# Which engine issues a load: 22 input loads move from SyncE's queue to ScalarE's in a recurrent-attention and mixer kernel

## The chip, the core and the metric

The kernel runs on one core of a Trainium2 chip. The metric is device time in microseconds of one execution, the median of several runs. Engines are named as in the profile: PE is TensorE's matmul, PEld its weight loads, DVE is VectorE, ACT is ScalarE, POOL is GpSimd, SP is SyncE. A q behind a name (SPq, ACTq) means the engine's sequencer.

## What is computed

Gated linear attention with a decay per key channel, then a mixer: a low-rank mix over the sequence with a residual, and a two-layer MLP with a residual. Inputs are float32, the output is float32 of shape 4 x 768 x 384.

```python
# q, k, v, alpha: (4 batches, 8 heads, 768 steps, 48 channels)
state = np.zeros((B, H, D, D))
for t in range(S):
    state = alpha[:, :, t, :, None] * state + einsum('bhd,bhe->bhde', k[:, :, t], v[:, :, t])
    y[:, :, t] = einsum('bhd,bhde->bhe', q[:, :, t], state)
x = y.transpose(0, 2, 1, 3).reshape(B, S, H * D)          # (4, 768, 384)
h = x.transpose(0, 2, 1) @ U @ V                          # U 768 x 32, V 32 x 768
u = x + h.transpose(0, 2, 1)
out = u + np.maximum(u @ w_ch1, 0) @ w_ch2                # w_ch1 384 x 1536, w_ch2 1536 x 384
```

## The kernel before

The sequence of each batch is cut in chunks of 128 steps, six to a batch. A unit "b.c" is chunk c of batch b; in batch 0 (all six) and batch 1 (the first four) two chunks are handled together as a pair, four heads at a time, and unit b.c is then one half of the heads of a pair. Each unit has four loads of 192 KB, one each of alpha, k, q and v, into one of 40 buffers of the pool io. For a unit:

- ACT takes the logarithm of alpha (L353, L524), PE sums it along the chunk with a triangular matrix (L362 to L369, L531 to L533), and ACT takes exp of the sum and of its negative (L376, L377, L541, L542; results aa, ai) and of the chunk's total (tot: L378, L544).
- k times ai and q times aa (rkq: L384, L552, on POOL or DVE) are transposed on PE (L401, L565) and copied to SBUF (kqt: L264 on ACT, L266 on DVE); in batch 3 a transposing DMA from SP does both (L577).
- PE makes the scores (L425, L593), DVE masks them (pm: L436, L603). v is cast to bf16 (rv: L264, L268). PE makes the state's update from rk and rv (L459, L616), DVE or POOL add and scale it (L474, L488, L627, L643), and PE makes y from scores and state (L498, L508, L655, L660).

Then the mixer of a batch runs: U and V (L675, L689), the sum u (L690), its transposes (L709, or a DMA from SP, L695), the first MLP matmuls (L738) with relu on ACT or DVE (L748, L750), the second (L764), the last sum (L770) and the stores (L773, L775). Weights are loaded and cast in pieces (L296, L264, L268).

The order of all this is written out. `Plan.add` collects some 1,050 operations with what each reads and writes. `TABLE` then lists them in the order in which they are emitted, three characters each: two for the operation's number and one for the engine (P PE, A ACT, D DVE, G POOL, S SP); "++B" is one matmul without use, which keeps PE running. `SLOTS` gives each buffer its place at first use. So every engine runs a fixed list in the table's order, and it waits where the next instruction of its list must wait, whatever stands behind it. All DMAs stand on SP's list: loads, stores and transposes, in the table's order. `Plan.run` calls each operation with its engine's name; a load ignores that name:

```python
P.add(f"load {b}.{c}", lambda e: nc.sync.dma_start(t(), src[b, :, sl, :].rearrange("h t d -> t h d")), w=[t])
```

The framework sets the semaphores. Each DMA gets one of eight landing semaphores in turn, in the order of emission; a DMA that takes a semaphore again waits until the DMA that had it before, eight places earlier, has landed.

At the start ACT loads its function table (L177) ahead of its first Ln. The first loads on SP's list are alpha 0.0, alpha 0.1, alpha 0.3, alpha 0.5, v 0.1, k 0.3, k 0.0, q 0.0, alpha 0.2, k 0.1, v 0.0, q 0.1.

Of the kernel before, what the change touches and what calls it, by code (L numbers as in the profile page):

```python
# [15 lines left out]
TABLE = """
A8SCcACePCfACgA++BBASCzABISDjA++BBQSETABDS++BBJSA9SA+SCiGBESCjG++BC0AChA++BC1PC2AC3ABBS++BA-SDlPDmADnADKA++BBCSCkPABSC5G
ClPCnABMSDoAEVPEXA++BC6DCmDBKSDCPDMPC4ABRSCdABLSBFSDOABUSAFGDPABSSD8ADDDC7PC9DCrPCsDBOSCoPDEPEWAC8PBHSCpDD+PC+ABNSCtPCqD
CvPCuDBGSDNADpGDrPC-PDqDCwPEZGDtADQGDkGDBDEbPEYAAJPDsPBTSDFDDyPGTAAKAEBACyADADDzPDuDD0DEaGEAAD-ADvPDxDAGPEcPAHAD1PEdDDGP
BWSDwDEeADHPDIDEDGEFPEHACxDGVPD2DDLGBYSBVSBPSGXADZPDaPDbDEfPECGDcPDRGGYAEUGDSPBXSDJDEEPD4PEiPEgDGWADdDALGDTPDUAAASD3PD5P  # L20
EhDEjPBcSEGADVAGaGD6AEIPGqAEkDEKDDWPElPDXDGZGBZSD7AGsPDePEmPGUGDfPELPD9AGtADYDEnPEoAEJDEMPENDDgPBaSDiAEpDBgSGbPGdAEOPBbS
GcPGeDEPPEQPERDGiPGjDDhAAOSADGAQSESAGfPAMSGgDEqPErPGwGHBAGvAGuAEsAHDPHGAGkDHFAE7PGhDE5PGyPGmPE8DE1PAWSGxGGnPHEAEtPEzPASS
G0AAUSE6DAeSE2DGzPAiSGrGE9PBdSAgSHaAAPGGoAEvPE0DE+AARGG1DGpAEuDBhSHcPHdAHeAEwDE3PBeSG2PE4DANGG5PExPG6DBkSFXPAYSBiSAcSG3D
G7DFYDFZPAXAAaSG4DFbPBfSATGEyAFcAFBPFCAAVGFdPFeAFJPFHPAhGFhPFKDFDPHHGAfAFiDAjAFRPFaAFFPFIABoSFVPFWAG8DHfAHJPHLAHIDHgDFGD
FSAE-PHiPHkDFfPHhGFEDFgDHKPHzAFtPAdAFrPBmSBlSBjSAoSFADHMAFuAAZABqSHjPHlDG9PG+PG-DAmSHAAHNPHPDAbGHCGAqSGlGHmPHQPAkSFsAAsS
H1PH3ABpSH5AFnPHRDHSGFLPHoDIJAH4AAuSAwSFjPH2AHODH7GFpPFkDAySILPFMDIMAINABnSHnDFPPH9PH-DHTDH6GFNPHbAFoAFqAH8PH+DFlPFmABrS
FQAFODHVPArAHWPHXPHpPHqDApGHYDA4SIAPHuPHZDIBDIPGIRPFTPAnGHrGAlAIOGHvPFvPHsDAtAHtDICDITDFUAF1PGHPIQPISDACSGNPIUPA2SA0SAzA
HwPAvGAxGGOPA6SHxAGBPIWDHUGIVDH0AAEGIDPB8SIHPIIAIKAIEDIFDGIPF2PB0SIGDIXPHyAA5AFwPIYAIZPGCPIaAIhPBwSIjPA3GBsSIbPA1GIiDIkD
B4SA7GGPPGDPIcDBvSIdPIeDFxPIpPIqDBtSGQDGEDGJPKTAKVPLSAInPKWAJ-AB+SIoDIlPIfPImACCSIgDKoAF3PF4DIrPIsDKBPKCABuSGKDKGDIzPB6S
BySKqPKAAI0AKuAJFPFyDKXAAIGKDAB1SJVPJWAIxPKbGKHGJGAJPPJQAKZAJDPCASJJPK9AJKABzSJEAJXPIyDJLPJMAKFAKEAI3PI7PKYAI8AI4AKrAJbP  # L30
JBPKUGKPPJYAI1PKsAK-PLBAB9SJZPLUPB2SJcDKtABxSKdPKQDLnAJRPJaAI-PLDAJSAKwGI2DKvDLAAJCDKaGLXAJHPJIDCESLYAJAAItPLVALZGIuAIvP
IwAKxPKzDKIPI5PKKDLWAI6ANWALCACGSI9PKyPI+AKJPKfDK0AKjPKkDKcPB3SJjPJkPB7SKLDLFGKMPLaGKeACBSKlGK+GKODK1PK2DKgPKiDJlPLpPLqA
NYPK3DNaANbAKpGB5SCDSF7PF8PB-SNeGLEGLbPJNPNcAKNDNZAKhDK4PLrALtGK7PLdALcPLsDK5DK6GCFSLeAF9PLHPLuPLJDCMSJOAKmPCISF+DLNPLwA
LODCUSK8AJTPJUALGPLIDLvPNdGLxACYSLPGCQSKRPKnANfSJ1PKSDJmDCLSNnALfPLgDLKPLLDLyPOdAJ2PLhDCHSLMDLTGLiPLjDLkGJ3PNpPOfPOiALoA
OLACKSNsAN5ANtAJvPL0DLlPLzDNrALQPLRDLmDJ6PL1PCaSJwPL2ANqANgPNvGL3PCJSL4AONPOOANXGOQANhDJ7PMAPL+POPANiDORACTSNuGJ8PMBDOhA
CSSL7PL-DMCSL8DNoAOvAL5PJpPL6DJdPL9SNjPNkDJxPCNSJqPMFPMGDCRSNwSJyDCWSJ9DJrPN7PN+AMDPMEDMHSJsDJePJfPN9AJ4DJgDOlGN0PN1DOMA
MKPMePNlPMLANmDMIPN8AMUPMVAOADMfAMJAN2GMWPCPSOSDMOPMYPMZACOSOgAMQPMRAOTDOUSCVSN-AMXAOxPOyAMPAMcPMaPMbDCZSMSPOkGOzAOBDMsP
MkPMlAMMPJiSMtDOCSMwPMgPMTAMxDN6AMdAMmPMnDMoPMpDOYPOjAOVPMyPOWDO0GMNDM0PM1AOGPOHDOmSOXDO1GMuPCXSMiPMjDMqPMhDMvDM4POIGOZD
ObPCbSO2SOaGM5PMzAOnPJhSOcAODPMrAF-SOoDNxPOEDF6SJ5SNyDF5SJoSNRPNSPM6POeAOFDOqPJtSO3PNzDOJPNHPOrDNIPGRSOpDOKAOtPOuAN3PM2P
OsGO4DOwGO5DN4DO6PO7ANCPO8PO9ANDPM7DM3DNJPPIPPJDPDPPKPPFPPGDNMPO+PNTPPEDNNPNOPGGSNKDPLDO-DJuSPHSPMSNEPNPDPAPPBDM9PM+PM-P  # L40
PzPNUDP1PGASP5PP6APrPPsAPtPPnPPoDPuDNFDPCSPdPPeAPTPNLSPUDP2APxPJ+SP0APvPPRPJ0SPXPPyDPfPPpPPSANVSPbPPcDPjPPkAPlPPmDNADPNP
GLSM8SPOAPVPPgDPYAP7PP8DPZPPPPJzSPqAQWPPwDQXPGSSQbPNGSNQSGMSP3PQMPJnSQNPP4DF0SNBSQcPGFSPWAFzSPQDQCPQYPPaDPhPPiDQHPQIPQJP
QKDQLSQdPQeDQfSP9PQDPQEPQZDQaSQFDQGSP+PQOPQPDP-PQRPQSPQADQTPQQSQBSQUDQVS
"""
# [94 lines left out]
def kernel(  # L139
# [37 lines left out]
    nc.scalar.preload_act_table_set("natural_log_exp_and_others")  # L177
# [84 lines left out]
    def copy(eng, dst, src):  # L262
# [4 lines left out]
        else:  # L267
            nc.gpsimd.tensor_copy(dst, src)  # L268
# [48 lines left out]
    def stage_loads(b):  # L317
        def load(t, src, c):
            if paired(b, c):
                hs, sl = slice((c % 2) * HP, (c % 2 + 1) * HP), slice((c // 2) * 2 * C, (c // 2 + 1) * 2 * C)  # L320
                P.add(
                    f"pload {b}.{c}",
                    lambda e: nc.sync.dma_start(  # L323
                        t().rearrange("p (h j) d -> p h (j d)", j=2), src[b, hs, sl, :].rearrange("h (p j) d -> p h (j d)", j=2)
                    ),
                    w=[t],
                )
# [2 lines left out]
            P.add(f"load {b}.{c}", lambda e: nc.sync.dma_start(t(), src[b, :, sl, :].rearrange("h t d -> t h d")), w=[t])  # L330
# [498 lines left out]
```

## Time and profile before

| | us |
|---|---|
| median of 3 runs | 160.46 |
| lowest and highest run | 160.12, 161.29 |
| span of the profiled execution, first to last instruction | 158.9 |
| PE busy in it | 149.6 (94%) |
| DVE busy | 105.2 (66%) |
| ACT busy | 90.7 (57%) |
| POOL busy | 60.0 (38%) |
| DMA queue q1, share of 16 engines | 86.7% |
| 120 loads (alpha, k, q, v, weights), each | 192 KB, 3.7 to 4.1 median to landing |

How to read the lines below. A line of the sums by stage has the stretch, its length, the busy time and the count of instructions of PE, PEld, DVE, ACT and POOL, the TensorE clock granted (1.00 is full), the mean busy share of the 16 DMA engines (packets that overlap can make it more than 1) and GB/s. A line of a timeline has the start in us, the length in us, engine, line, operation, what it writes and reads with its shape, how many were merged, and in brackets the idle time of the engine before it with what ended it. SPq lines are the issues: the time that SP's sequencer took to issue, not the transfer.

### The profile page before, as it was taken

How to read it: one execution, taken by the hardware profiler on the slowest of the kernel's cores; microseconds unless marked ns; L12 is line 12 of the kernel's file. 1: busy time of each engine (PE TensorE's matmuls, PEld its weight loads, DVE VectorE, ACT ScalarE, POOL GpSimd, SP SyncE). 2: the span in 40 equal slices, each digit the busy share in tenths (PEclk: the TensorE clock that was granted, in tenths of full speed). 3: DMA queues.
4: the chain of work that ended last, by engine and by line, in shares of the span. 5: the costliest groups of instructions: out<-in, count | busy, mean ns of one | idle time of the engine just before them, and what ended most of it. 6: DMA issues, size and time to landing. Idle time of an engine off the chain costs nothing.

```text
span 158.9 us, 4479 instructions
## 1 busy us (share of the span) xinstructions
PE 149.6 (94%) x1712; PEld 98.0 (62%) x1712; DVE 105.2 (66%) x236; ACT 90.7 (57%) x233; POOL 60.0 (38%) x95
## 2 busy tenths in 40 slices
...
GB/s 137 284 295 311 277 198 271 274 273 240 241 257 305 212 241 215 188 207 215 219 159 196 160 222 142 150 186 219 153 194 181 99 75 209 262 132 69 0 154 143
DMA packets 99364, 31.64 MB, mean 199 GB/s; under 512 B 93040, under 2 KB 99312, under 8 KB 99344
## 3 DMA queue, kind: packets, MB, share of 16 engines
q1 hardware_dynamic: 99344, 31.37, 86.7%
...
## 4 chain that ended last, share of the span: by engine, by line
PE 71%; DMA 12%; SPq 6%; POOL 3%; issue 3%; ACT 2%; DVE 0%; POOLq 0%; ACTq 0%
PE ps L764 29%; PE ps L738 20%; SPq L323 6%; DMA io<-in_k_dram 4%; DMA io<-in_v_dram 3%; PE ps L689 3%; DMA kqt<-rkq 3%; DMA io<-in_moe_w_ch_dram 2%; PE ps L593 2%; PE ps L565 2%; PE ps L660 2%; PE ps L401 2%; PE ps L709 1%; PE ps L531 1%; PE ps L655 1%
## 5 line engine op out<-in xcount | busy, mean ns | idle before, releaser
L764 PE MATMUL ps<-w_sb,h1t 128*128 128x384 bf16 (+2 forms) x300 | 53.1, 319 | 0.1
L738 PE MATMUL ps<-uT,w_sb 128*128 128x384 bf16 x288 | 51.0, 326 | 0.0
L748 ACT ACTIVATE h1t<-ps 128x384 bf16<-128x384 f32 x58 | 27.1, 507 | 19.1 <-PE ps L738 19.1
L764 PEld LDWEIGHTS <-h1t 128*128 128x128 bf16 x300 | 27.3, 97 | 16.1 <-issue 0.8
L738 PEld LDWEIGHTS <-w_sb 128*128 128x128 bf16 x288 | 27.0, 98 | 16.1 <-issue 0.2
L750 DVE TENSOR_SCALAR h1t<-ps 128x384 bf16<-128x384 f32 x38 | 19.8, 551 | 19.0 <-PE ps L738 19.0
L552 POOL TENSOR_TENSOR rkq<-io,aa 128x384 bf16<-128x384 f32 x12 | 11.2, 939 | 26.3 <-ACT h1t L748 12.6
L603 DVE TENSOR_TENSOR pm<-ps,maskc 128x512 bf16<-128x512 f32 x28 | 17.7, 681 | 3.7 <-PE ps L593 3.7
L690 DVE TENSOR_TENSOR ub<-xb,ps 128x384 bf16<-128x384 bf16 x24 | 12.2, 548 | 6.9 <-PE ps L689 6.9
L770 DVE TENSOR_TENSOR io<-ub,ps 128x384 f32<-128x384 bf16 (+2 forms) x25 | 12.9, 532 | 3.7 <-PE ps L764 3.6
L436 DVE TENSOR_TENSOR pm<-ps,maskp 128x512 bf16<-128x512 f32 x20 | 13.2, 683 | 0.2
L264 ACT CAST xb<-ps 128x192 bf16<-128x192 f32 (+1 forms) x21 | 8.2, 392 | 9.1 <-PE ps L660 5.5
L264 ACT COPY kqt<-ps 128x512 bf16<-128x512 bf16 x18 | 10.4, 605 | 3.1 <-PE ps L401 1.9
L384 POOL TENSOR_TENSOR rkq<-io,ai 128x384 bf16<-128x384 f32 x9 | 8.2, 914 | 6.3 <-DMA io<-in_k_dram 4.5
L552 POOL TENSOR_TENSOR rkq<-io,ai 128x384 bf16<-128x384 f32 x9 | 8.1, 913 | 5.7 <-DMA io<-in_k_dram 5.5
L627 POOL TENSOR_TENSOR st<-sm,tot 128x384 bf16<-128x384 f32 x8 | 6.6, 828 | 8.0 <-DVE sm L643 8.0
L541 ACT ACTIVATE ai<-ps 128x384 bf16<-128x384 f32 x14 | 7.0, 502 | 4.1 <-PE ps L531 2.4
L266 DVE COPY kqt<-ps 128x512 bf16<-128x512 bf16 x18 | 7.4, 420 | 2.8 <-PE ps L565 2.0
L401 PE MATMUL ps<-ident,rkq 128*128 128x128 bf16 x80 | 7.8, 224 | 1.2 <-POOL rkq L384 1.2
L268 POOL CAST w_sb<-io 128x384 bf16<-128x384 f32 x14 | 6.8, 505 | 5.5 <-DMA io<-in_moe_w_ch_dram 5.5
L544 ACT ACTIVATE tot<-ps,off 128x4 f32<-128x4 f32 x22 | 5.6, 279 | 5.3 <-PE ps L533 3.4
L524 ACT ACTIVATE lt<-io 128x384 bf16<-128x384 f32 x14 | 7.4, 540 | 1.5 <-DMA io<-in_alpha_dram 1.5
(108 smaller groups left out, 220.7 us busy)
## 6 DMA issues: line engine op xcount, KB each, us to landing
...
```

What stands on the lines that cost most here:

```text
L264: nc.scalar.copy(dst, src)
L323: lambda e: nc.sync.dma_start(t().rearrange("p (h j) d -> p h (j d)", j=2), src[b, hs, sl, :].rearrange("h (p j) d -> p h (j d)", j=2)),
L401: nc.tensor.matmul(dst, lhsT=ring()[:, HP * j + 2 * a : HP * j + 2 * a + 2, :].rearrange("t h w -> t (h w)"), rhs=ident, start=True, stop= ...
L436: nc.vector.tensor_tensor(dst, s2, maskp.to_broadcast([C, 2, 2, C]), op=ALU.mult)
L552: eng.tensor_tensor(dst()[:, :, 0:D], a(), x(), op=ALU.mult)
L603: nc.vector.tensor_tensor(pm()[:, :, par, :], s2, maskc.to_broadcast([C, HP, C]), op=ALU.mult)
L690: P.add(f"u {b}.{c}", lambda e, c=c, hb=hb: nc.vector.tensor_tensor(ub()[:, c, :], xb()[:, c, :], hb()[:, 0:DM], op=ALU.add), r=[hb] + xk( ...
L738: nc.tensor.matmul(hb()[:, 0:TW], lhsT=w1_sb[:, ct, jt * 128 : (jt + 1) * 128], rhs=u_half(uT, ct, tt, b in QUEUE_U), start=(ct == 0), sto ...
L748: nc.scalar.activation(dst, hb()[:, 0:TW], AF.Relu)
L750: nc.vector.tensor_scalar_max(dst, hb()[:, 0:TW], 0.0)
L764: nc.tensor.matmul(hb()[:, 0 : hi - lo], lhsT=h1()[:, jt, c * C : (c + 1) * C], rhs=w2_sb[:, jt, lo:hi], start=(jt == 0), stop=(jt == NJ - 1),
L770: P.add(f"out_{hi - lo} {b}.{c}", lambda e, hb=hb, lo=lo, hi=hi: nc.vector.tensor_tensor(flat(ou)[:, lo:hi], ub()[:, c, lo:hi], hb()[:, 0 ...
```

## The change

Loads are issued by the engine that the table names, SP or ACT, through a new function `queue`. In the table 22 loads are given to ACT:

- alpha 0.1 and alpha 0.5 move to the front of the table, and the function table's load becomes an operation of the table, right behind them;
- q 0.1, k 0.5, alpha 1.0, v 0.2, v 0.5, k 1.0, alpha 1.2 and alpha 1.3 stay at their place in the table and now stand in ACT's list there;
- v 2.0 to 2.5 and v 3.0 to 3.5 likewise.

All other operations, their engines, order and buffers are the same.

```diff
-    nc.scalar.preload_act_table_set("natural_log_exp_and_others")
...
+    def queue(eng):
+        return nc.scalar if eng == "ACT" else nc.sync
...
-        P.add("wload", lambda e: nc.sync.dma_start(flat(t), src), w=[t])
+        P.add("wload", lambda e: queue(e).dma_start(flat(t), src), w=[t])
...
                     f"pload {b}.{c}",
-                    lambda e: nc.sync.dma_start(
+                    lambda e: queue(e).dma_start(
...
-            P.add(f"load {b}.{c}", lambda e: nc.sync.dma_start(t(), src[b, :, sl, :].rearrange("h t d -> t h d")), w=[t])
+            P.add(f"load {b}.{c}", lambda e: queue(e).dma_start(t(), src[b, :, sl, :].rearrange("h t d -> t h d")), w=[t])
...
             mlp2(b, ub, h1, c)
+    P.add("table", lambda e: nc.scalar.preload_act_table_set("natural_log_exp_and_others"))
     P.run("".join(TABLE.split()), "".join(SLOTS.split()))
```

The start of the table, and one of the loads that stay at their place (q 0.1, operation "BC"):

```diff
-A8SCcACePCfACgA++BBASCzABISDjA++BBQSETABDS++BBJSA9SA+SCiGBESCjG++BC0AChA++BC1PC2AC3ABBS++BA-SDlPDmADnADKA++BBCSCkPABSC5G
+BAABQAQgAA8SCcACePCfACgA++BCzABISDjA++BETABDS++BBJSA9SA+SCiGBESCjG++BC0AChA++BC1PC2AC3ABBS++BA-SDlPDmADnADKA++BBCACkPABS
```

More of the change, by code (lines that the diff above doesn't have):

```diff
@@ L16 @@
 TABLE = """
-A8SCcACePCfACgA++BBASCzABISDjA++BBQSETABDS++BBJSA9SA+SCiGBESCjG++BC0AChA++BC1PC2AC3ABBS++BA-SDlPDmADnADKA++BBCSCkPABSC5G
-ClPCnABMSDoAEVPEXA++BC6DCmDBKSDCPDMPC4ABRSCdABLSBFSDOABUSAFGDPABSSD8ADDDC7PC9DCrPCsDBOSCoPDEPEWAC8PBHSCpDD+PC+ABNSCtPCqD
-CvPCuDBGSDNADpGDrPC-PDqDCwPEZGDtADQGDkGDBDEbPEYAAJPDsPBTSDFDDyPGTAAKAEBACyADADDzPDuDD0DEaGEAAD-ADvPDxDAGPEcPAHAD1PEdDDGP
-BWSDwDEeADHPDIDEDGEFPEHACxDGVPD2DDLGBYSBVSBPSGXADZPDaPDbDEfPECGDcPDRGGYAEUGDSPBXSDJDEEPD4PEiPEgDGWADdDALGDTPDUAAASD3PD5P
@@ L21 @@
[L21 to L40, printed above, removed]
@@ L41 @@
-PzPNUDP1PGASP5PP6APrPPsAPtPPnPPoDPuDNFDPCSPdPPeAPTPNLSPUDP2APxPJ+SP0APvPPRPJ0SPXPPyDPfPPpPPSANVSPbPPcDPjPPkAPlPPmDNADPNP
-GLSM8SPOAPVPPgDPYAP7PP8DPZPPPPJzSPqAQWPPwDQXPGSSQbPNGSNQSGMSP3PQMPJnSQNPP4DF0SNBSQcPGFSPWAFzSPQDQCPQYPPaDPhPPiDQHPQIPQJP
-QKDQLSQdPQeDQfSP9PQDPQEPQZDQaSQFDQGSP+PQOPQPDP-PQRPQSPQADQTPQQSQBSQUDQVS
+BAABQAQgAA8SCcACePCfACgA++BCzABISDjA++BETABDS++BBJSA9SA+SCiGBESCjG++BC0AChA++BC1PC2AC3ABBS++BA-SDlPDmADnADKA++BBCACkPABS
+C5GClPCnABMSDoAEVPEXA++BC6DCmDBKSDCPDMPC4ABRACdABLSBFSDOABUAAFGDPABSSD8ADDDC7PC9DCrPCsDBOSCoPDEPEWAC8PBHACpDD+PC+ABNSCtP
@@ new lines @@
+CqDCvPCuDBGSDNADpGDrPC-PDqDCwPEZGDtADQGDkGDBDEbPEYAAJPDsPBTADFDDyPGTAAKAEBACyADADDzPDuDD0DEaGEAAD-ADvPDxDAGPEcPAHAD1PEdD
+DGPBWSDwDEeADHPDIDEDGEFPEHACxDGVPD2DDLGBYSBVABPSGXADZPDaPDbDEfPECGDcPDRGGYAEUGDSPBXSDJDEEPD4PEiPEgDGWADdDALGDTPDUAAASD3P
+D5PEhDEjPBcAEGADVAGaGD6AEIPGqAEkDEKDDWPElPDXDGZGBZSD7AGsPDePEmPGUGDfPELPD9AGtADYDEnPEoAEJDEMPENDDgPBaSDiAEpDBgAGbPGdAEOP
+BbSGcPGeDEPPEQPERDGiPGjDDhAAOSADGAQSESAGfPAMSGgDEqPErPGwGHBAGvAGuAEsAHDPHGAGkDHFAE7PGhDE5PGyPGmPE8DE1PAWSGxGGnPHEAEtPEzP
+ASSG0AAUSE6DAeSE2DGzPAiSGrGE9PBdSAgSHaAAPGGoAEvPE0DE+AARGG1DGpAEuDBhSHcPHdAHeAEwDE3PBeSG2PE4DANGG5PExPG6DBkSFXPAYSBiSAcS
@@ new lines @@
+G3DG7DFYDFZPAXAAaSG4DFbPBfSATGEyAFcAFBPFCAAVGFdPFeAFJPFHPAhGFhPFKDFDPHHGAfAFiDAjAFRPFaAFFPFIABoSFVPFWAG8DHfAHJPHLAHIDHgD
+FGDFSAE-PHiPHkDFfPHhGFEDFgDHKPHzAFtPAdAFrPBmSBlSBjSAoSFADHMAFuAAZABqSHjPHlDG9PG+PG-DAmSHAAHNPHPDAbGHCGAqSGlGHmPHQPAkSFsA
+AsSH1PH3ABpSH5AFnPHRDHSGFLPHoDIJAH4AAuSAwSFjPH2AHODH7GFpPFkDAySILPFMDIMAINABnSHnDFPPH9PH-DHTDH6GFNPHbAFoAFqAH8PH+DFlPFmA
+BrSFQAFODHVPArAHWPHXPHpPHqDApGHYDA4SIAPHuPHZDIBDIPGIRPFTPAnGHrGAlAIOGHvPFvPHsDAtAHtDICDITDFUAF1PGHPIQPISDACSGNPIUPA2SA0S
+AzAHwPAvGAxGGOPA6SHxAGBPIWDHUGIVDH0AAEGIDPB8SIHPIIAIKAIEDIFDGIPF2PB0SIGDIXPHyAA5AFwPIYAIZPGCPIaAIhPBwSIjPA3GBsSIbPA1GIiD
@@ new lines @@
+IkDB4SA7GGPPGDPIcDBvAIdPIeDFxPIpPIqDBtSGQDGEDGJPKTAKVPLSAInPKWAJ-AB+SIoDIlPIfPImACCSIgDKoAF3PF4DIrPIsDKBPKCABuSGKDKGDIzP
+B6SBySKqPKAAI0AKuAJFPFyDKXAAIGKDAB1SJVPJWAIxPKbGKHGJGAJPPJQAKZAJDPCASJJPK9AJKABzAJEAJXPIyDJLPJMAKFAKEAI3PI7PKYAI8AI4AKrA
+JbPJBPKUGKPPJYAI1PKsAK-PLBAB9SJZPLUPB2SJcDKtABxSKdPKQDLnAJRPJaAI-PLDAJSAKwGI2DKvDLAAJCDKaGLXAJHPJIDCESLYAJAAItPLVALZGIuA
+IvPIwAKxPKzDKIPI5PKKDLWAI6ANWALCACGSI9PKyPI+AKJPKfDK0AKjPKkDKcPB3AJjPJkPB7AKLDLFGKMPLaGKeACBSKlGK+GKODK1PK2DKgPKiDJlPLpP
+LqANYPK3DNaANbAKpGB5SCDAF7PF8PB-ANeGLEGLbPJNPNcAKNDNZAKhDK4PLrALtGK7PLdALcPLsDK5DK6GCFSLeAF9PLHPLuPLJDCMSJOAKmPCISF+DLNP
```

12 lines of the change are left out of this document (11 added, 1 removed).

## Prediction

> **What bounds the kernel now.** I read the page first, then the sums by stage, then the chain that ended last, and last the timelines of single engines.
>
> ```profile
> span 158.9 us, 4479 instructions
> core 0: us, PE busy (x) PEld busy (x) DVE busy (x) ACT busy (x) POOL busy (x), PEclk, DMA share, GB/s
> 0.00:8.00 8.00, 4.11 (x23) 2.17 (x24) 2.60 (x23) 4.67 (x10) 3.27 (x15) 1.00 0.81 211
> 8.00:20.00 12.00, 10.61 (x187) 7.23 (x186) 8.28 (x20) 9.70 (x27) 9.65 (x12) 0.93 1.09 294
> 20.00:32.00 12.00, 11.82 (x274) 9.09 (x272) 10.70 (x25) 10.36 (x29) 8.24 (x14) 0.93 0.91 249
> 32.00:60.00 28.00, 27.89 (x347) 18.15 (x344) 20.31 (x47) 19.34 (x49) 14.16 (x24) 1.00 0.98 251
> 60.00:110.00 50.00, 50.00 (x515) 33.15 (x514) 35.27 (x70) 37.05 (x101) 19.12 (x24) 1.00 1.05 190
> 110.00:120.00 10.00, 9.27 (x99) 5.75 (x96) 8.50 (x17) 2.85 (x8) 4.27 (x5) 1.00 1.06 177
> 120.00:150.00 30.00, 30.00 (x236) 18.64 (x236) 16.17 (x32) 6.77 (x15) 1.27 (x2) 1.00 0.49 132
> ```
>
> From 32 us on PE is full (27.89 of 28, 50.00 of 50, 30.00 of 30) except for 0.73 us around 115. PE runs a fixed list, so the kernel's length is the moment at which batch 0 has let PE into that full stretch, plus what PE still waits later. Up to 32 us no single engine is full: PE, DVE, ACT and POOL hand work round, and the DMA engines are saturated (share 1.09 from 8 to 20). An edit of loads can act in two places only: before 32, and in the few late waits. These are the rows before 32 that matter:
>
> ```profile
> 0.73 2.10 SPq L323 DMA_DIRECT2D io<-in_alpha_dram  x4
> 7.54 0.55 SPq L323 DMA_DIRECT2D io<-in_q_dram  x1
> 9.74 0.51 SPq L323 DMA_DIRECT2D io<-in_k_dram  x1
> 12.33 1.14 SPq L323 DMA_DIRECT2D io<-in_q_dram  x2
> 0.73 1.28 ACT L177 ACT_TABLE_LOAD   x1 [0.73 <-PEq L813]
> 3.31 0.52 ACT L353 ACTIVATE lt<-io 128x384 bf16<-128x384 f32 x1 [1.30 <-DMA io<-in_alpha_dram]
> 9.05 0.49 ACT L377 ACTIVATE aa<-ps 128x384 bf16<-128x384 f32 x1
> 9.42 0.52 ACT L353 ACTIVATE lt<-io 128x384 bf16<-128x384 f32 x1
> L353 ACTq EVENT_SEMAPHORE  x2: 17/17/17, 6.1 to 9.3; - x2
> 11.36 0.56 DVE L384 TENSOR_TENSOR rkq<-io,aa 128x384 bf16<-128x384 f32 x1 [7.17 <-DMA io<-in_q_dram]
> 11.84 0.42 DVE L266 COPY kqt<-ps 128x512 bf16<-128x512 bf16 x1
> 21.20 0.36 DVE L474 TENSOR_TENSOR st<-ps,tot 128x192 bf16<-128x192 f32 x1 [1.03 <-PE ps L459]
> 12.56 0.42 PE L425 MATMUL ps<-kqt 48*64 48x128 bf16 x16
> 17.05 0.42 PE L425 MATMUL ps<-kqt 48*64 48x128 bf16 x16
> 18.10 0.40 PE L401 MATMUL ps<-ident,rkq 128*128 128x128 bf16 x4 [0.37 <-POOL rkq L384]
> 17.13 0.91 POOL L384 TENSOR_TENSOR rkq<-io,aa 128x384 bf16<-128x384 f32 x1 [0.88 <-DMA io<-in_q_dram]
> DMA to landing us min/median/max: 2.6/3.8/4.7
> ```
>
> Read them so. SP needs 0.51 to 0.55 us per load and issues without a pause. DVE stands idle for 7.17 us until q 0.1 (batch 0, unit 1) has landed, and then works through a queue of things that PE needs: the copy at 11.84 feeds the score matmuls at 12.56. A second path through POOL waits for q 0.5 at 17.13 and lets PE go at 18.10.
>
> **The change, part by part.** It adds no work: 22 loads leave SP's list (10 pair loads, 12 v loads) and stand at the same places of ACT's, except alpha 0.1 and 0.5, which move to the very front, ahead of the table load. So a load now waits for all that ACT has ahead of it, and ACT's later instructions wait while it is issued. The program also gives each load one of eight landing semaphores in table order, whichever engine issues; a load waits until the one eight places before it has landed, so the two queues now wait for each other.
>
> *The first three alphas.* They are now issued at 0.73 side by side. Alpha 0.0 shares the DMA engines with 0.1, one more load of 192 KB in front of its landing. The 294 GB/s of the row from 8 to 20 makes that 196.6 KB / 294 = 0.67 us, so the first Ln comes between 3.31 and 3.98. The table load, two issues later, ends near 0.73 + 2 x 0.53 + 1.28 = 3.07, which is still under the wait of 1.30: nothing. On the DMA side SP gets two issues free (1.1 us), but the engines are the limit right after, so I count no gain. The later Ln is what q 0.1 queues behind, and that one waits for alpha 0.2, not for the first Ln: nothing more here.
>
> *Eight pair loads, in order q 0.1, k 0.5, alpha 1.0, v 0.2, v 0.5, k 1.0, alpha 1.2, alpha 1.3.* The one with a price is q 0.1. SP issued it at 7.54 and it let DVE go at 11.36, 3.82 us later. On ACT it stands behind the Ln of alpha 0.2. That Ln runs at 9.42, but its semaphore step is at 9.3, while the ACTIVATE of 9.05 is still running: ACT's sequencer runs ahead of the engine, so I let the load go at 9.35. Landing takes between the shortest latency of the trace, 2.6, and the 3.82 that this load had: 11.95 to 13.17 against 11.36. ACT's queue is empty, SP's is full, so I take a little over the middle, 3.3: 12.65, **1.3 us late on DVE**. Behind it in DVE's order stand the copies and masks of units 0 and 1; behind these, PE's scores at 12.56 and 17.05, both late by as much. At 18.10 PE had waited 0.37 for POOL anyway, so there the delay shrinks to 0.93. DVE's idle 1.03 at 21.20 doesn't take it up, since that was a wait for PE, which is itself late. After that DVE, busy 10.70 of 12 from 20 to 32, has no room to catch up before PE takes over: **+0.93** (bounds +0.2 and +1.4).
>
> k 0.5 goes from 9.74 to about 11: POOL's waits (0.88 at 17.13) cover its consumer. The other six land early enough for theirs. What all eight cost ACT is its sequencer: the trace has no DMA issue on ACT. By SP's rows it is 0.51 to 0.55 us, by the run-ahead above an ACTIVATE of 0.49 covers most of it. Bounds: nothing; and 8 x 0.55 = 4.4 us with no cover, against ACT's idle time of 24 - 9.70 - 10.36 = 3.94 us from 8 to 32, of which a fifth may lie where it is of no use: 4.4 - 3.2 = 1.2. I stay near the lower end, as the run-ahead is seen: **+0.2**.
>
> The Trainium skill, "DMA: Bandwidth & Descriptors", section "Issuing engines are not separate DMA queues", speaks against the change: loads started from several engines end on the same 16 DMA engines, and only sequencer time is saved. With the DMA share of 1.09 the trace agrees; by that rule the first part of the sum would be a loss alone, as I have it.
>
> *Twelve v loads of batches 2 and 3.* ACT has room in most places, not in one:
>
> ```profile
> 70.00:80.00 10.00, 10.00 (x111) 6.85 (x108) 5.25 (x12) 9.31 (x29) 6.47 (x9) 1.00 1.09 215
> 74.18 1.51 SPq L330 DMA_DIRECT2D io<-in_v_dram  x2
> 78.13 1.20 ACT L264 COPY kqt<-ps 128x512 bf16<-128x512 bf16 x2
> 79.31 0.84 PE L593 MATMUL ps<-kqt 48*128 48x128 bf16 x24
> 80.34 0.95 POOL L268 CAST rv<-io 128x384 bf16<-128x384 f32 x2
> 83.19 0.33 PE L616 MATMUL ps<-rv,rkq 128*128 128x96 bf16 x4
> ```
>
> v 2.2 and v 2.3 now stand between the two copies of 78.13, 1.51 us of issue in an ACT that is busy 9.31 of 10. If the sequencer came to them only with the first copy, the second would end 1.0 later (79.33 to 80.4) and PE's scores of 79.31 would wait 0.6. If it runs ahead as at 9.3, nothing. They land some 3.8 after 78, POOL's casts of 80.34 move to about 82.3, and PE's L616 at 83.19 still finds them. I take **+0.2** (0 to +0.6).
>
> Late, the loads that leave SP do help:
>
> ```profile
> 105.24 0.58 SPq L330 DMA_DIRECT2D io<-in_v_dram  x1
> 108.43 1.22 SPq L330 DMA_DIRECT2D io<-in_k_dram  x2
> 111.79 1.78 POOL L552 TENSOR_TENSOR rkq<-io,ai 128x384 bf16<-128x384 f32 x2 [3.67 <-DMA io<-in_k_dram]
> 115.28 0.33 PE L655 MATMUL ps<-st,kqt 128*128 128x96 bf16 x4 [0.24 <-POOL st L627]
> 116.95 0.84 PE L593 MATMUL ps<-kqt 48*128 48x128 bf16 x24 [0.48 <-DMA kqt<-rkq]
> ```
>
> SP works without a pause from 105.24 to the k load of 108.43, on which POOL and then the DMA transpose and PE wait. v 3.2 gone, that k is issued about 0.6 earlier, and the 0.48 at 116.95 goes: **-0.5** (0 to -0.8 with the 0.24 of 115.28).
>
> **Sum:** 0.93 + 0.2 + 0.2 - 0.5 = +0.83 us on the span of 158.9. The median of the runs is 160.46, 1.56 more than the span, which holds what lies around it. Forecast 160.46 + 0.83 = **161.3 us**. By the bounds it is 160.46 + 0.2 - 0.8 = 159.9 to 160.46 + 1.4 + 1.2 + 0.6 = 163.7.
>
> **Rivals.** *A, ACT becomes the bound of batch 0: 162.8.* Both queues may not prepare loads at once, so an issue on ACT would first wait for SP's, which runs nearly always: 0.55 + up to 0.51 less 0.4 of cover, 8 times, 5.3 us, against ACT's idle 3.94. The 1.3 over is PE's delay: 0.93 + 1.3 + 0.6 - 0.5 = +2.3. It decides when an issue on ACT takes over 0.9 us. For it: ACT and PE pass work back and forth all through 8 to 32. Against: no row shows an issue on ACT.
>
> The Trainium skill, again "DMA: Bandwidth & Descriptors", section "Queues, rings and completion order", says that SP and ACT own a ring each but no descriptor generator of their own; no run here shows it, and if it holds, this rival does.
>
> *B, the queues stop each other: 162.8.* By the eight semaphores SP can't issue q 0.5 until q 0.1 has landed, and a weight load near 30 us until alpha 1.3 has. With five loads fewer ahead of it SP comes to q 0.5 at 12.33 - 5 x 0.55 = 9.6. If q 0.1 lands only at 13.2, SP stands for 3.6 us; what is in flight lasts for less, and the DMA engines run dry for some 0.7 us, as again at 30: 0.93 + 1.4 = +2.3. It decides when q 0.1 lands after 13. Against: with 3.8 us to landing and 0.55 per issue six or seven loads are in flight when SP stops, and from 20 to 32 the DMA share is 0.91, not full.
>
> *C, the other side, not slower: 159.4.* Two alphas fewer ahead of alpha 0.2 on SP are 1.1 us. If the DMA engines can follow, alpha 0.2 lands that much earlier, the semaphore step of 9.3 is at 8.2, and q 0.1, alone in ACT's queue, lands 2.6 us later at about 10.9: DVE loses nothing. q 0.5, with fewer loads ahead of it on SP, ends POOL's 0.88 earlier and PE's 0.37 at 18.10 goes: 160.46 - 0.37 - 0.7 late = 159.4. It decides when DVE's first multiply starts before 11.4. For it: SP's issue time is the only thing that goes down. Against: the share of 1.09, which leaves nothing for an earlier landing.
>
> **How the numbers follow.** The forecast has 0.45 (its own range 160.5 to 162.1), A 0.22, B 0.13, C 0.20. The runs before lie 0.7% apart, so 1% (158.86 to 162.06) is about what can be told from no change. Faster by over 1% needs C and 0.5 us more: 0.10. Slower by over 1% is A and B with the edge of the forecast: 0.37. Within 1%: 0.53. The range, 159.0 to 163.7, reaches from a little below C to the upper bound of the sum.
>
> **What would show it.** Right: L177 at about 1.8 and the first Ln at 3.3 to 4.0; DVE's first L384 near 12.7 with a DMA of q ahead of it; no wait for a DMA at 116.95's place; ACT's issues about 0.55 us each; the windows after 32 as full as now. C is right if that L384 starts before 11.4. A shows in issues of 0.9 us and more on ACT and an ACT without idle time from 8 to 32; B in holes in SP's list and a lower DMA share from 10 to 14 and near 30. I'd be wrong altogether if PE got new waits of over 0.5 us each between 40 and 110.

## The result and the profile after

The changed kernel takes **165.49 us** (164.92 to 167.08, 4 runs) against 160.88 (160.12 to 161.33) of the kernel before in the same rounds: ratio **1.0316** (95% interval 1.0249 to 1.0384), +4.6 us where +0.83 was forecast. It is slower, and beyond the range of 159.0 to 163.7. The profiled execution has a span of 163.1 us, 4.2 more than before. Some runs of one kernel come out over 1.5% above its fastest: the ratios here and below leave them out, the medians don't, and e4 and e10 have no ratio because too few of their runs are left.

The sums by stage of the kernel after, columns as before:

```profile
8.00:20.00 12.00, 9.51 (x166) 6.50 (x164) 6.13 (x15) 8.49 (x24) 7.55 (x10) 1.00 1.11 298
20.00:32.00 12.00, 10.40 (x259) 8.03 (x258) 10.62 (x25) 9.72 (x28) 8.28 (x13) 1.00 0.93 264
...
60.00:110.00 50.00, 48.06 (x505) 31.82 (x500) 34.91 (x68) 33.74 (x91) 17.74 (x22) 1.00 0.92 171
...
86.00:91.00 5.00, 3.89 (x69) 3.28 (x69) 2.97 (x6) 3.37 (x8) 5.00 (x6) 1.00 0.05 11
```

PE was busy for less time in both places where loads were moved: 10.61 - 9.51 = 1.1 us from 8 to 20, 11.82 - 10.40 = 1.4 from 20 to 32, and 1.94 in the stretch 60 to 110, which had been full. The clock is 1.00 throughout, so nothing is lost to a low clock. Before 32 us the busy times can't be compared as they stand, since the kernel before had a clock of 0.93 there and was busy longer with the same matmuls; the lateness below is the better measure. From 86 to 91 the DMA engines stand nearly still (share 0.05). The next view lists what PE waited for, in us in total, number of waits and the longest; these are its new rows of over 0.5 us:

```profile
...
PE ps L460 <- DVE kqt L264: 1.9, 1, 1.9
PE ps L617 <- POOL rv L266: 1.3, 1, 1.3
PE ps L739 <- DMA uT<-ub: 0.8, 1, 0.8
PE ps L765 <- DVE sm L644: 0.6, 1, 0.6
...
```

None of the four was there before, and the wait of 0.48 for a DMA of kqt is gone. (After's line numbers are one higher.) PE's list is the same, so its lateness can be read off the same matmul in both traces. First rows of the timeline of PE before, then of after:

```profile
21.10 0.64 PE L425 MATMUL ps<-kqt 48*64 48x128 bf16 x16
50.16 0.65 PE L764 MATMUL ps<-w_sb,h1t 128*128 128x384 bf16 x3
86.73 0.65 PE L764 MATMUL ps<-w_sb,h1t 128*128 128x384 bf16 x3
```

```profile
19.97 0.40 PE L402 MATMUL ps<-ident,rkq 128*128 128x128 bf16 x4
22.01 0.42 PE L426 MATMUL ps<-kqt 48*64 48x128 bf16 x16
27.69 0.40 PE L402 MATMUL ps<-ident,rkq 128*128 128x128 bf16 x4 [0.53 <-POOL rkq L385]
51.88 0.65 PE L765 MATMUL ps<-w_sb,h1t 128*128 128x384 bf16 x3
86.49 0.33 PE L617 MATMUL ps<-rv,rkq 128*128 128x96 bf16 x4 [1.31 <-POOL rv L266]
90.81 0.81 PE L765 MATMUL ps<-w_sb,h1t 128*128 128x384 bf16 x4 [0.62 <-DVE sm L644]
121.02 0.79 PE L594 MATMUL ps<-kqt 48*128 48x128 bf16 x22
```

PE is 1.87 late at 18.10 (19.97), **1.72** at 50.16 (51.88), **3.30** at 83.19 (86.49), **4.08** at 86.73 (90.81) and still 4.07 at 116.95 (121.02): there the new 0.77 for uT, at 112.62, has been paid back by the late waits that went. So some 1.7 us is lost with batch 0, 2.4 around 85, nothing later on balance. The 1.7 understates what the waits cost: at 21.10 (22.01) PE is only 0.91 late, because the kernel before ran at its low clock there (the same 16 matmuls took 0.64 us before and 0.42 after). New waits behind that, 0.53 at 27.69 and 0.49 at 29.45 among them, raise the lateness again.

What stands behind the waits, from the timelines of ACT, SP, DVE and POOL:

```profile
9.62 0.37 ACTq L324 DMA_DIRECT2D io<-in_q_dram  x1
13.37 0.56 DVE L385 TENSOR_TENSOR rkq<-io,aa 128x384 bf16<-128x384 f32 x1 [9.16 <-DMA io<-in_q_dram]
13.90 0.37 SPq L324 DMA_DIRECT2D io<-in_alpha_dram  x1
18.12 0.92 SPq L324 DMA_DIRECT2D io<-in_v_dram  x2
21.32 0.47 ACTq L324 DMA_DIRECT2D io<-in_k_dram  x1
26.72 0.91 POOL L385 TENSOR_TENSOR rkq<-io,ai 128x384 bf16<-128x384 f32 x1 [2.03 <-DMA io<-in_k_dram]
75.90 4.71 SPq L331 DMA_DIRECT2D io<-in_alpha_dram  x5
79.39 0.38 ACTq L331 DMA_DIRECT2D io<-in_v_dram  x1
79.81 0.60 ACTq L331 DMA_DIRECT2D io<-in_v_dram  x1
85.48 0.96 POOL L266 CAST rv<-io 128x384 bf16<-128x384 f32 x2 [3.25 <-DMA io<-in_v_dram]
91.06 1.34 SPq L578 DMA_TRANSPOSE kqt<-rkq  x1
DMA to landing us min/median/max: 4.4/5.0/5.6
```

q 0.1 leaves at 9.62, and DVE's first multiply starts at 13.37 instead of 11.36. SP issues nothing between 13.90 and 18.12. k 1.0 leaves at 21.32, and POOL stands idle 2.03 us for it. In the middle SP, without its v loads, runs ahead through five alphas of batch 3 from 75.90 on, while v 2.2 and v 2.3 leave ACT at 79.39 and 79.81 and take 4.4 and 5.6 us (the last line, for these two), where SP had issued them at 74.18 and 74.95. POOL starts its casts at 85.48, not 80.34. SP's next instruction, a transpose that needs POOL, comes only at 91.06; hence the empty DMA engines. SP's own waits say it too:

```profile
SPq L578 <- POOL rv L266: 10.7, 1, 10.7
...
SPq L324 <- DMA io<-in_alpha_dram: 4.2, 2, 3.8
```

The second of these (3.8 us at once) is a load of SP that has to take a landing semaphore which alpha 1.0, on ACT, still holds. Which load takes which semaphore is the framework's own choice: it is not the order of emission that the section on the kernel gives (the load at 18.12 comes two DMAs behind alpha 1.0 in the table, not eight), though a DMA does wait for the last one that had its semaphore.

### The profile page after: what moved, and what is told of

Same layout as the page of the kernel before. It is cut to its first block, busy times and chain, and to the rows that moved or that the text cites. A ratio compares the mean times of both kernels' runs of the same rounds, so it can differ in the third digit from the quotient of the medians.

```text
span 163.1 us, 4470 instructions
## 1 busy us (share of the span) xinstructions
PE 148.6 (91%) x1712; PEld 97.6 (60%) x1712; DVE 106.6 (65%) x236; ACT 90.4 (55%) x233; POOL 61.1 (37%) x95
## 4 chain that ended last, share of the span: by engine, by line
PE 74%; DMA 13%; issue 4%; DVE 3%; POOL 3%; ACT 1%; POOLq 0%; DVEq 0%; ACTq 0%
PE ps L765 26%; PE ps L739 25%; DMA io<-in_alpha_dram 4%; DMA io<-in_k_dram 3%; DMA uT<-ub 3%; PE ps L690 2%; DMA io<-in_q_dram 2%; PE ps L594 2%; PE ps L566 2%; PE ps L402 2%; PE ps L255 2%; PE ps L661 2%; PE ps L656 1%; PE ps L710 1%; DVE io L771 1%
## 5 line engine op out<-in xcount | busy, mean ns | idle before, releaser
L553 POOL TENSOR_TENSOR rkq<-io,aa 128x384 bf16<-128x384 f32 x12 | 11.2, 941 | 24.7 <-DMA io<-in_q_dram 11.9
L385 POOL TENSOR_TENSOR rkq<-io,ai 128x384 bf16<-128x384 f32 x9 | 8.6, 960 | 8.7 <-DMA io<-in_k_dram 5.3
L553 POOL TENSOR_TENSOR rkq<-io,ai 128x384 bf16<-128x384 f32 x9 | 8.5, 949 | 4.7 <-DMA io<-in_k_dram 3.7
L266 POOL CAST rv<-io 128x384 bf16<-128x384 f32 x12 | 6.2, 522 | 6.6 <-DMA io<-in_v_dram 6.6
L385 POOL TENSOR_TENSOR rkq<-io,aa 128x384 bf16<-128x384 f32 x7 | 6.4, 914 | 4.7 <-DMA io<-in_q_dram 2.4
```

What stands on the lines that cost most here:

```text
L385: eng.tensor_tensor(jh(dst()[:, :, 0:D]), raw(a), jh(x()), op=ALU.mult)
L553: eng.tensor_tensor(dst()[:, :, 0:D], a(), x(), op=ALU.mult)
```

## The experiments

Two theories were tried. *Place*: a moved load costs by how much later ACT comes to it than SP did. *Sharing*: two queues on the same DMA engines cost, or let SP put less urgent bytes in front, whatever the place. Ratios are against the kernel before, run on the same chip (its medians: 160.46 to 160.63). The last column has the TensorE clock granted in the profiled execution from 8 to 20 and from 20 to 32 us; for the kernel before it is 0.93 and 0.93, for after 1.00 and 1.00.

| run | what | median us | ratio (95%) | span of the profile | clock |
|---|---|---|---|---|---|
| e1 | after, 12 v loads back on SP | 163.99 | 1.0198 (1.0072 to 1.0324) | 161.4 | 1.00, 1.00 |
| e2 | only the 12 v loads moved | 165.18 | 1.0282 (1.0164 to 1.0401) | 163.5 | 1.00, 1.00 |
| e3 | only the two alphas moved | 160.17 | 1.0026 (0.9987 to 1.0064) | 159.3 | 1.00, 1.00 |
| e4 | only the eight pair loads moved | 165.55 | - | 163.0 | 0.86, 1.00 |
| e5 | only v 3.0 to 3.5 moved | 161.46 | 1.0064 (1.0021 to 1.0108) | 157.8 | 1.00, 1.00 |
| e6 | after, v 2.2 and 2.3 back | 165.04 | 1.0199 (1.0075 to 1.0324) | 164.2 | 0.86, 1.00 |
| e7 | after, q 0.1 back | 165.16 | 1.0286 (1.018 to 1.0392) | 163.6 | 0.88, 0.83 |
| e8 | e2, v 2.2 and 2.3 earlier on ACT | 160.72 | 1.0055 (1.0015 to 1.0095) | 158.4 | 1.00, 1.00 |
| e9 | after, alpha 1.0 back | 167.7 | 1.0412 (1.0327 to 1.0498) | 165.7 | 0.84, 0.73 |
| e10 | after, q 0.1 and alpha 1.0 back | 166.61 | - | 165.2 | 0.86, 0.86 |
| e11 | e2, six loads of SP cut to an eighth | 161.59 | 1.0073 (1.004 to 1.0107) | 160.5 | 1.00, 0.86 |
| e12 | after, v 2.2 and 2.3 earlier on ACT | 164.69 | 1.023 (1.0142 to 1.0317) | 162.3 | 0.86, 0.86 |
| e13 | e1, eight pair loads earlier on ACT | 160.85 | 1.0027 (0.9981 to 1.0073) | 158.1 | 1.00, 1.00 |
| e14 | after, all ten of these earlier on ACT | 161.46 | 1.0048 (1.0006 to 1.009) | 160.2 | 1.00, 1.00 |
| e15 | only alpha 1.0 moved | 161.18 | 1.0067 (1.0022 to 1.0112) | 158.6 | 1.00, 1.00 |
| e16 | only q 0.1 moved | 165.35 | 1.0332 (1.026 to 1.0404) | 164.1 | 0.79, 0.64 |

Edits are in the table: two characters for the load, then S or A.

**The parts.** e1 gives the v loads back, e2 moves them alone, e3 the alphas alone, e4 the pair loads alone.

```diff
 e1, from after; e2 has the other loads back instead
-B3A ... B7A ... CHA        (v 2.2, v 2.3, v 3.0, and the other nine)
+B3S ... B7S ... CHS
 e3 and e4 likewise: only BAA BQA (alpha 0.1, 0.5), only BCA BRA BUA BHA BTA BVA BcA BgA (pair loads)
```

> The change without the twelve v loads (they are SP's again). Theory 1, each load costs by its place in ACT's list, so the three groups add up: PE's lateness of 1.7 us at 50 us stays, what came at 83 to 91 (+2.4) and at 112 (+0.9) goes, and so does the gain at 117 (-0.95): 160.5 + 1.7 = 162.2. Rival 2, the eight shared semaphores hold both queues wherever one of them is late: the early stop of SP (13.9 to 18.1 us) is then most of the loss and this stays near 164.

> The twelve v loads of batches 2 and 3 alone on ACT, everything else as before. Theory 1: +2.4 + 0.9 - 0.95 = +2.3, so 162.8, with the wait of POOL for v near 80 us as in the changed kernel. Rival 2: without the early stop the queues are in step again and little is lost: 160.5 or, with the gain at 117, 159.6.

> Alpha 0.1 and 0.5 alone go to ACT, ahead of the table load. Theory 1: the first Ln is 0.6 us later (3.9), later loads on SP come up to 1.1 us earlier, q 0.1 is issued by SP near 6.5 and DVE starts near 10.5 instead of 11.4: between -0.5 and +0.3, 160.0 to 160.8. A rival, that the first Ln sets all of batch 0: +0.6, 161.1.

> The eight pair loads from q 0.1 to alpha 1.3 alone go to ACT; alphas 0.1 and 0.5 and all v loads stay on SP. Theory 1: q 0.1 lands about 2 us later than before, DVE and PE with it, and k 1.0 adds to that at 27 us: +1.2 to +2.0, 161.7 to 162.5. Rival 2, SP held by ACT's loads is what counts: about the same time, but with DVE's first multiply on time and the loss only after 14 us.

The alphas cost nothing that can be told (1.0026). The pair loads with them (e1) and the v loads alone (e2) each cost over 3 us, both more than was expected. They don't add up: in e2 and in after POOL gets v 2.3 at nearly the same moment (the rows of e2 below, and 85.48 above), and a PE that is late already loses less to it. Of e4's four runs one, with a granted clock of 0.998 over its span, took 162.22, within the range of the first theory; the other three had 0.957 to 0.990 and took 164.78 to 167.81, so e4 settles little.

**The v loads of batch 2.** e5 moves only batch 3's, e6 puts v 2.2 and v 2.3 of after back on SP, e8 leaves both on ACT but five ACTIVATEs and a copy earlier, e11 leaves their places in both lists and takes bytes away, e12 is e8's edit in the whole change.

```diff
 e5, from e2: v 2.0 to 2.5 back
-B3A ... B7A
+B3S ... B7S
 e6, from after: the same two alone
-B3A ... B7A
+B3S ... B7S
 e8 from e2, e12 from after
-LWAI6ANWALCACGSI9PKyPI+AKJPKfDK0AKjPKkDKcPB3AJjPJkPB7A
+B3AB7ALWAI6ANWALCACGSI9PKyPI+AKJPKfDK0AKjPKkDKcPJjPJkP
 e11, from e2
+nh = 1 if b == 3 and ((src is k and c == 0) or (src is alpha and c > 0)) else H
-... queue(e).dma_start(t(), src[b, :, sl, :].rearrange("h t d -> t h d")), w=[t])
+... queue(e).dma_start(t()[:, 0:nh, :], src[b, 0:nh, sl, :].rearrange("h t d -> t h d")), w=[t])
-... nc.scalar.activation(lt()[:, :, 0:D], at(), AF.Ln), r=[at], w=[lt])
+... AF.Ln, scale=0.0 if b == 3 and c > 0 else 1.0, bias=1.0 if b == 3 and c > 0 else 0.0), r=[at], w=[lt])
```

> Only the six v loads of batch four are ACT's; all else is as before. Theory 1 (a load costs by its place in its engine's list and by what SP does meanwhile): nothing changes until 88 us, so the whole loss of the v-only kernel at 83 (PE +3.7) is absent, and the end stands at 159.5 to 161.0: the late stall of 0.48 on k 3.4 may go, the wait for tu at 107 to 112 us may still grow by up to 0.9. Rival (any load on a second queue costs, because two queues share the DMA engines): half of the v-only kernel's loss of 4.7, so about 162.8.

> The changed kernel with v 2.2 and v 2.3 on SP again at their old place. Theory 1: the PE wait at 83 us, which grew PE's lateness from 1.7 to 4.1, goes; the end is 162.5 to 163.5. Rival (it is not these two, SP runs ahead whenever any v load of batch three leaves it, and v 2.4 or v 2.5 take their place as the late ones): 164.5 to 165.5, with a PE wait of over 1.5 us on POOL's rv between 83 and 92.

> Only the twelve v loads on ACT, as in the v-only kernel, but v 2.2 and v 2.3 stand five ACTIVATEs earlier in ACT's list, at about 76 us instead of 78.35 and 78.77. If the place alone counts, they land 3.8 after their issue, by 80.5, POOL's casts stand as before (80.34) and the v-only kernel's loss of 3.7 at 83 us is gone: 161.0 to 162.0. If it is the two queues sharing the DMA engines once SP has run ahead, they take 5.7 and 7.0 as they did there, land at 81.7 and 83.5, and PE still loses 1.5 to 2.5: 162.8 to 164.0.

> The v-only kernel (v 2.2 and v 2.3 at 78.35 and 78.77 in ACT's list, landing 5.72 and 7.03 later), with the loads k 3.0 and alpha 3.1 to 3.5, which SP issues around them, cut to one of their six heads, and those alphas' logarithms taken of a constant: their place in both lists is the same, their bytes are a sixth. If the bytes that SP had put ahead in the DMA engines are what makes the two loads late, they take about 3.8 again, land by 82.2 and 82.8, and the PE wait at 83 us (3.67) shrinks to under 1: the end at 161.0 to 162.2. If their place in ACT's list is enough by itself, the loss stays above 2.5 and the end at 163.8 to 165.2.

> The changed kernel whole, but with v 2.2 and v 2.3 five ACTIVATEs earlier in ACT's list, as in the v-only kernel where that took the loss away. If the two parts add, the early 2.4 stay and the mid 2.4 with the wait at 112 go: 162.5 to 163.5. If the early lateness shifts which loads are late, so that others hold POOL at 83 to 92 us, 164.5 to 165.5.

e11 leaves out seven of the eight heads in these six loads (the expectation speaks of six heads), and takes the logarithms of alpha 3.1 to 3.5 of a constant. Timelines of ACT, POOL and PE with the latency of the two loads, first e2, then e8, then e11 (whose lines are one higher again):

```profile
78.35 0.37 ACTq L331 DMA_DIRECT2D io<-in_v_dram  x1
85.85 0.95 POOL L266 CAST rv<-io 128x384 bf16<-128x384 f32 x2 [4.61 <-DMA io<-in_v_dram]
86.86 0.33 PE L617 MATMUL ps<-rv,rkq 128*128 128x96 bf16 x4 [2.66 <-POOL rv L266]
DMA to landing us min/median/max: 5.7/6.4/7.0
```

```profile
75.56 0.37 ACTq L331 DMA_DIRECT2D io<-in_v_dram  x1
81.07 0.95 POOL L266 CAST rv<-io 128x384 bf16<-128x384 f32 x2 [1.04 <-DMA io<-in_v_dram]
82.87 0.33 PE L617 MATMUL ps<-rv,rkq 128*128 128x96 bf16 x4
DMA to landing us min/median/max: 4.0/4.5/5.0
```

```profile
78.81 0.37 ACTq L332 DMA_DIRECT2D io<-in_v_dram  x1
83.30 0.95 POOL L266 CAST rv<-io 128x384 bf16<-128x384 f32 x2 [1.61 <-DMA io<-in_v_dram]
84.49 0.33 PE L618 MATMUL ps<-rv,rkq 128*128 128x96 bf16 x4
DMA to landing us min/median/max: 3.9/4.0/4.0
```

Either remedy is enough. 2.8 us earlier in ACT's list (e8), PE doesn't wait, and the kernel is back within 1%; the loads also land 1.7 to 2 us faster there. At the same late place but with little else in the DMA engines (e11) they take 3.9 and 4.0, as on SP (3.8 and 3.9 before), and PE doesn't wait either. So the 2.66 of e2 is two delays in a row: 4 us of place, which POOL's and PE's slack just took in e11, and 2 to 3 us of transfer behind what SP had put ahead. Neither theory is right alone. e5 shows that batch 3's v loads were not the cause. They are no gain either: the profiled span is short, the runs are not (1.0064, a little above the range expected). In the profiles of e6 and e12 PE has no wait for POOL's rv, so the part comes off the whole change as well. Their ratios (1.0199, 1.023) point the same way, to about what e1 leaves, but with intervals that reach 1.032 they can't be told apart from the whole change's 1.0316; both profiles also have a low clock in batch 0 (0.86 from 8 to 20), which after does not have.

**The early loads.** e7, e9 and e10 put q 0.1, alpha 1.0 and both back on SP; e13 gives all eight pair loads an earlier place in ACT's list, e14 all ten; e15 and e16 leave one late load alone on ACT.

```diff
 e7 (q 0.1), e9 (alpha 1.0), e10 (both), from after
-BCA ... BUA
+BCS ... BUS
 e13, from e1; e14, from after with e8's edit too. q 0.1 as an example, the other seven likewise
-ChA++BC1PC2AC3ABBS++BA-SDlPDmADnADKA++BBCA ...
+BCAChA++BC1PC2AC3ABBS++BA-SDlP ...
 e15, from before: only BUS becomes BUA. e16, from before: only BCS becomes BCA
```

> The changed kernel with q 0.1 on SP again. If the early lateness is q 0.1's place behind Ln 0.2 (theory 1), the PE wait at 12.31 of 2.0 us goes and the end is 163.0 to 164.2. Rival (the stop of SP from 13.9 to 18.1 us, behind alpha 1.0 on ACT, sets the early lateness anyway): PE is again 1.5 to 2 late by 31 us and the end is 164.8 to 165.8.

> The changed kernel with alpha 1.0 on SP again. Theory S (the stop of SP behind alpha 1.0's landing, from about 14 to 18 us, sets the early lateness): that stop goes, but q 0.1 still makes PE wait 2 us at 12.31, so it is only the following loads that come sooner; PE's lateness at 50 us is 0.5 to 1.5 instead of 2.4, the end 163.8 to 164.8. Rival (the stop costs nothing beside q 0.1): the lateness stays at 1.7 to 2.4 and the end at 165.0 to 165.8.

> The changed kernel with q 0.1 and alpha 1.0 both on SP again. With q 0.1 alone back, PE lost its 2 us at 16.7 instead of at 12.31, while SP stood from 12.7 to 17.7 behind alpha 1.0. Theory S: with both back neither wait is there, PE is at most 0.7 late at 31 us and the end is 162.6 to 163.8, the v loads' part alone. Rival (the early lateness comes from having any of the eight pair loads on ACT): 1.5 to 2.5 late at 31 us, the end at 164.6 to 165.6.

> The changed kernel without its v loads (two alphas and eight pair loads on ACT, 1.02 times the kernel before with them at their late places), but each pair load stands a few ACTIVATEs earlier in ACT's list, so that ACT comes to it about when SP did in the kernel before: q 0.1 at 7.5 us instead of 9.6, alpha 1.0 at 11.2 instead of 14.05. If the places make the early loss (directly, or through SP that stands behind a late one's landing), SP's stop of 3.8 us and PE's wait of 1.9 at 12.31 go: 160.2 to 161.4. If sharing eight pair loads between two queues costs whatever their place, 162.8 to 164.5.

> The changed kernel whole, with the eight pair loads and v 2.2 and v 2.3 at those earlier places of ACT's list; the same loads are ACT's. If place is what the change lost by, it is within 1 per cent of the kernel before: 159.8 to 162.0. If not, 163 or more.

> The kernel before with alpha 1.0 alone on ACT, at its late place in ACT's list. If a single late load is enough to stop SP behind its landing, SP stands for 3 to 4 us between 11 and 19 us and PE is 1 to 2.5 late by 31 us: 161.6 to 163.0. If it takes several, nothing: 160.0 to 160.9.

> The kernel before with q 0.1 alone on ACT, behind Ln 0.2, at 9.4 to 9.7 us. The prediction's price for it was 0.93 at the end. If it is what its own lateness makes, PE waits for DVE's kqt at 12.31 by 1.3 to 2.0 us and the end is 161.3 to 162.6. If that wait is soaked up by the waits that follow it (PE's 0.37 at 18.10 and those for loads after it), 160.2 to 161.0.

By the medians, taking single loads back was no remedy. e7 came out as its rival had it (1.0286): q 0.1's wait was gone, but PE stood 1.2 us, until 18.62, for another result of ACT's. e9 and e10 missed both their ranges. Part of this is the clock, which fell in batch 0 of all three profiles and not in that of after. The only run of e7 and the only one of e10 with a granted clock of 1.000 over the span took 163.09 and 163.38, within the ranges of the theory (163.0 to 164.2, 162.6 to 163.8). So what q 0.1 is worth in the whole change stays open. SP's stop did not go in e9 and e10; it went to the next load of ACT that held a semaphore. The longest row of SP's waits for a DMA in e9 and in e10:

```profile
SPq L324 <- DMA io<-in_v_dram: 3.9, 2, 3.2
```

```profile
SPq L324 <- DMA io<-in_k_dram: 6.5, 2, 3.7
```

But the stop is not itself the price. In e15, with alpha 1.0 alone on ACT, SP stood as well:

```profile
SPq L324 <- DMA io<-in_alpha_dram: 2.8, 1, 2.8
```

and the kernel lost 0.7%: 161.18, between the two ranges expected (up to 160.9 without effect, from 161.6 with it), and a profiled span no longer than before (158.6, at a clock of 1.00 instead of 0.93 up to 32 us). Alone on ACT, q 0.1 costs far more. e16, its ACT, DVE and PE rows, its sums by stage (now only PE) and its PE waits:

```profile
9.37 0.42 ACTq L324 DMA_DIRECT2D io<-in_q_dram  x1
14.54 0.56 DVE L385 TENSOR_TENSOR rkq<-io,aa 128x384 bf16<-128x384 f32 x1 [10.35 <-DMA io<-in_q_dram]
15.89 0.64 PE L426 MATMUL ps<-kqt 48*64 48x128 bf16 x16
29.19 0.64 PE L426 MATMUL ps<-kqt 48*64 48x128 bf16 x32
...
8.00:20.00 12.00, 8.15 (x127) 0.79 1.04 273
20.00:32.00 12.00, 11.70 (x218) 0.64 0.98 279
...
PE ps L460 <- DVE kqt L264: 2.8, 1, 2.8
```

And the row of the kernel before that belongs to the second of these PE rows:

```profile
23.39 0.85 PE L425 MATMUL ps<-kqt 48*64 48x128 bf16 x32
```

One load of 192 KB, issued at 9.37 instead of 7.54, and the kernel is 3.3% slower, as much as with the whole change. The load took 5.1 us to land, DVE began 3.2 us late, PE waited 2.8 at 12.31's place, and the span grew by 5.2. But this is not all q 0.1's wait: PE is 3.33 late at 12.56 (15.89) and 5.80 at 23.39 (29.19). The 2.5 between lie in a stretch with a granted clock of 0.79 and 0.64 instead of 0.93 and 0.93; that the clock fell because of the wait was not tried. All four runs of e16 had a granted clock of 0.958 to 0.969 over the span, those of after 0.987 to 1.000, so e16 can't stand for q 0.1's share of the change: in the profile of after PE waited 1.9 and the clock stayed at 1.00. The Trainium skill, "TensorE: Matmul & The Clock Gate", section "HAM oscillation — how this bites in real kernels", puts the limit of a harmless gap at about 3.4 us. No such limit comes out of these traces: the clock fell after a wait of 2.8 in e16, with none over 1.2 between the start and 32 us in e7 and none over 0.5 there in the kernel before, and it did not fall after one of 1.9 in after.

With the places mended the loss is gone. e13's rows of ACT, DVE and PE:

```profile
5.97 0.42 ACTq L324 DMA_DIRECT2D io<-in_q_dram  x1
10.12 0.56 DVE L385 TENSOR_TENSOR rkq<-io,aa 128x384 bf16<-128x384 f32 x1 [5.91 <-DMA io<-in_q_dram]
...
PE ps L363 <- ACT lt L354: 5.1, 2, 4.4
...
```

q 0.1 left at 5.97, DVE started at 10.12, 1.24 earlier than before, and PE's wait for DVE's kqt is not in its list: behind the 4.4 at the very start nothing is over 0.7 us. The kernel is as fast as before (1.0027), with ten loads on ACT. e14, with all 22 on ACT, is at 1.0048: of the 3.2% of the change 2.7 were the places of ten loads. These comparisons, e1 with e13, e2 with e8 and after with e14, are the ones that carry the argument: in all six profiles the clock is 1.00 from 8 to 32. No version beat the kernel before.

## Why the prediction was wrong, point by point

- **Base and alphas: right; ACT's own cost: no run takes it apart.** PE full from 32 us on was the right view. Alpha 0.1 and 0.5 are worth nothing (e3), as said. ACT's issues took 0.37 to 0.47 us for the pair loads, all but one beside an ACTIVATE or a COPY, 0.60 at most for the v loads above, never over 0.9: **A is wrong**. Whether +0.2 was enough stays open: PE has new waits for ACT of 0.37 at 19.07 and 0.49 at 29.45, and no run tells whether the issues made them. Of a descriptor generator that both queues share, which the Trainium skill states ("DMA: Bandwidth & Descriptors", section "Queues, rings and completion order"), nothing shows in these times.
- **q 0.1, +0.93: mechanism right, size wrong.** The issue was forecast for 9.35 and came at 9.62 (9.37 in e16). The step that failed is the landing, "between 2.6 and 3.82", with 3.3 taken because ACT's queue is empty: it was 3.7 in after, longer than 3.3 but within the bounds, and 5.1 in e16, beyond them. An empty queue of its own did not make the load faster here, with the DMA engines' share at 1.11 and 1.04. DVE came 2.01 late in after instead of 1.3, and PE's wait was 1.9 there and 2.8 in e16. At the matmul of 18.10, for which +0.93 was worked out, PE was 1.87 late in after, above the upper bound of 1.4. e16's price of over 5 us, with the stretch of low clock in it, was in none of the cases.
- **"The other six land early enough for theirs": wrong.** The rows of before for k 1.0, SP's issue and POOL's product with it:

```profile
18.12 0.55 SPq L323 DMA_DIRECT2D io<-in_k_dram  x1
22.86 0.91 POOL L384 TENSOR_TENSOR rkq<-io,ai 128x384 bf16<-128x384 f32 x1
```

  From 18.12 to 22.86 there are 4.7 us, and a load takes 3.8: a slack of 0.9. On ACT k 1.0 left at 21.32, 3.2 later, and took 5.2 to land. That cost POOL 2.03 and PE 0.53 at 27.69. The slack could have been read before; only q 0.1's and k 0.5's were.
- **v 2.2 and v 2.3, +0.2: the largest miss.** The step was "they land some 3.8 after 78". They left at 79.39 and 79.81, took 4.4 and 5.6, and POOL's casts came at 85.48, 3.2 later than the 82.3 of the prediction. PE lost 2.4 (4.08 - 1.72). The prediction asked what the issues do to ACT and took the latency of SP's queue; it did not ask what SP would do with the time it was given. SP went on to alphas of batch 3, and those bytes stood in the engines ahead of, or beside, v 2.3. That such bytes make these two loads late was shown by e11, with the v loads alone on ACT.
- **Late, -0.5: right in kind.** The 0.48 for kqt went, and a new 0.77 for uT came. That transpose took 4.8 us instead of 3.2, with v 3.2 issued beside it; no run takes that apart, and it stays open.
- **B: the mechanism is there, the price was not.** SP stood for 3.8 us in after, behind alpha 1.0 and not q 0.1, and 2.8 in e15, where the kernel lost 0.4 to 1.8 us in all (1.0022 to 1.0112). The eight places of the semaphores that B starts from are not what the framework does, as said above. As a cause of the loss the stop comes behind the late loads themselves.
- **C: wrong as it stands.** DVE started at 13.37, not before 11.4. e13 made its condition true (10.12), and still there was no gain beyond 1%. The Trainium skill's rule in "DMA: Bandwidth & Descriptors", section "Issuing engines are not separate DMA queues", that a second issuing engine saves sequencer time at most, agrees with e13.
- **"Wrong altogether if PE got new waits of over 0.5 us each between 40 and 110"**: it got two, 1.31 and 0.62, and one of 0.77 just after, at 112.62.
